# A leaky ramp on ScalarE in place of a byte comparison on VectorE, and a new order for the start of an attention and feed-forward kernel

## The chip, the cores and the metric

One core of one Trainium2 chip runs the whole program in one launch. The metric is the device time of that launch in microseconds (us). All matrix products are float32; a product with full precision is made of three products of 128x128 by up to 288 columns (high by high, low by high, high by low), since each operand is split into a part that TensorE keeps and a rest.

## What is computed

Memory attention (8 batches, 8 heads, 576 positions, 64 wide, 32 memory slots), then two feed-forward blocks:

```
a = softmax(phi, over 32 slots)          # [b, h, s, m]
k_m, v_m = a^T k, a^T v                  # [b, h, m, d]
x = softmax(q k_m^T / 8) v_m             # -> [b, s, 512]
xk = mu_k*x + (1-mu_k)*x_prev            # x_prev: x one position earlier
xr = mu_r*x + (1-mu_r)*x_prev
x2 = sigmoid(xr w_r) * (relu(xk w_k)^2 w_v)
u, v = relu(x2 w_in) halves;  v = layer_norm(v)
out = (u * (w_spatial v + b_spatial)) w_out
```

The weights arrive as 64-bit floats, bit for bit, and the kernel turns them into float32 itself.

## The kernel before

**Units.** The work goes through 16 half blocks `i` (batch `b`, half `hf` of 288 positions). In each, TensorE makes 8 key products (`w_k`, tiles W1h and W1l), 4 gate products (`w_r`, W2h and W2l) and 4 value products (`w_v`, W3h and W3l), L616 to L690; then the second feed-forward block follows (L699 on). Attention runs in 16 groups `i` of 4 heads (`att_step`, L212): a reduction and an exponential of phi, the memory's keys and values (L235, 20 rows of small products), their transposition (L273), the scores (L285), a second softmax on VectorE and ScalarE (L291 to L317), and the products that write x (L337 to L342, tile xT).

**Weights.** `load_f64` (L109) takes one unit of 128x512 64-bit numbers: a DMA into one of four staging buffers (st0, st1 and two halves of xT1, in turn), a scaling on ScalarE of the upper words (L123), the lowest bits of the lower words by ScalarE (L127, first 6 units) or VectorE (L129), a comparison on VectorE of the sign's byte, which writes 128 or 0 into the byte that holds the sign (L131), a shift and OR on VectorE (L135), a rounded copy on ScalarE (L141) and the rest on VectorE (L142). w_k has 8 units, w_r 4, w_v 8; 12 more (w_in, w_out) come in the middle of the run.

**Order.** Up to the first half block the text is written out by the string `ORDER` (L34): capitals and small letters of A, C, K, Q (group 0) and B, D, L, R (group 1) are input loads, `w` is one unit of w_k, `a` and `b` take the two first attention groups one stage on. `FIRST_BLOCK` (L37) does the same inside half block 0. From then on `pump` (L357) is called 20 times per half block, and takes the following attention groups on by 0, 2 or 1 steps. A scheduler then moves instructions within each engine's queue, and each queue runs strictly in its order. DMAs of this kernel all go through SyncE's queue, in its order too.

Of the kernel before, what the change touches and what calls it, by code (L numbers as in the profile page):

```python
# [8 lines left out]
F32 = mybir.dt.float32  # L9
F32R = mybir.dt.float32r  # L10
U32 = mybir.dt.uint32
U8 = mybir.dt.uint8
ACTF = mybir.ActivationFunctionType
ALU = mybir.AluOpType
# [5 lines left out]
DM, DFF = 512, 1024  # L20
# [8 lines left out]
KC = DM // 128  # L29
# [1 line left out]

ORDER = "AICKMBDwLQRwwqwraaawaaabbbabaabbwbbwbw"  # L34


FIRST_BLOCK = ["arxxab", "b", "rxabr", "xab", "", "", "", "rv", "vvvv", "v", "", "vv"]  # L37
# [3 lines left out]
def kernel(  # L41
# [18 lines left out]
    nc = tc.nc  # L60
    scale = 1.0 / float(D) ** 0.5
# [44 lines left out]
    stages = []  # L106
    units = [0]

    def load_f64(src, wh=None, wl=None, raw=None):  # L109


        c, f = src.shape[1], src.shape[2] // 2
        buf = stages.pop(0)
        stages.append(buf)
        if isinstance(buf, str):
            buf = tile_of(buf, [128, 1024], U32)
        st = buf[:, 0:2 * c * f].rearrange("p (c f b) -> p c f b", c=c, b=2)
        nc.sync.dma_start(out=st.rearrange("p c f b -> p c (f b)"), in_=src)
        low, top = st[:, :, :, 0], st[:, :, :, 1]
        by = buf.bitcast(U8)[:, 0:8 * c * f].rearrange("p (c f b) -> p c f b", c=c, b=8)  # L120


        nc.scalar.activation(out=top.bitcast(F32), in_=top.bitcast(F32), func=ACTF.Copy, scale=2.0**-112)  # L123
        units[0] += 1
        if units[0] <= 6:

            nc.scalar.activation(out=low, in_=by[:, :, :, 3], func=ACTF.Copy, scale=2.0**-5, bias=-0.4999)  # L127
        else:
            nc.vector.tensor_scalar(out=low, in0=low, scalar1=29, scalar2=None, op0=ALU.logical_shift_right)  # L129

        nc.vector.tensor_scalar(  # L131
            out=by[:, :, :, 3], in0=by[:, :, :, 7], scalar1=128.0, scalar2=128.0, op0=ALU.is_ge, op1=ALU.mult
        )
        out = top if raw is None else raw.bitcast(U32)
        nc.vector.scalar_tensor_tensor(  # L135
            out=out, in0=top, scalar=3, in1=low, op0=ALU.logical_shift_left, op1=ALU.bitwise_or
        )
        v = out.bitcast(F32)
        if wh is None:
            return v  # L140
        nc.scalar.activation(out=wh, in_=v, func=ACTF.Copy)  # L141
        nc.vector.tensor_tensor(out=wl, in0=v, in1=wh.bitcast(F32), op=ALU.subtract)  # L142

    def weight(src, dst, n_c, width):

        chunks = src.bitcast(U32).rearrange("(c p) f -> p c f", p=128)
        for f0 in range(0, width, 128):
            for c in range(0, n_c, 4):
                load_f64(
                    chunks[:, c:c + 4, 2 * f0:2 * f0 + 256],  # L150
                    dst[0][:, c:c + 4, f0:f0 + 128], dst[1][:, c:c + 4, f0:f0 + 128],
                )
                yield
# [58 lines left out]
    def att_step(i):  # L212
        b, g = divmod(i, G)
        sp = space(i)
        pT, ph, kv, q, st, mx, rs, sm = sp.pT, sp.ph, sp.kv, sp.q, sp.st, sp.mx, sp.rs, sp.sm
# [10 lines left out]
            out=ph, in0=ph, in1=bc[:, None, :].to_broadcast([128, NT, 128]), op=ALU.subtract  # L226
# [6 lines left out]
        for t in range(NT):  # L233
            for j in range(HG):
                nc.tensor.matmul(  # L235
                    out=kvp[32 * j:32 * j + 32, :], lhsT=ph[:, t, 32 * j:32 * j + 32],
                    rhs=kv[:, t, j, :], start=(t == 0), stop=(t == NT - 1),
                )
            if t == 1:
                yield True  # L240
        nc.vector.tensor_scalar(out=rs, in0=kvp[:, 128:129], scalar1=1e-9, scalar2=None, op0=ALU.add)
        nc.vector.reciprocal(out=rs, in_=rs)

# [1 line left out]
            out=km.rearrange("p (e d) -> p e d", e=2), in0=kvp[:, None, 0:64].to_broadcast([128, 2, 64]),  # L245
            scalar1=rs, scalar2=None, op0=ALU.mult,
        )
        if wide:
            nc.vector.scalar_tensor_tensor(
                out=vb, in0=kvp[:, None, 64:128].to_broadcast([128, HG, 64]), scalar=rs,  # L250
                in1=mask_sb[:, 2:, None].to_broadcast([128, HG, 64]), op0=ALU.mult, op1=ALU.mult,
            )
            x = vb.rearrange("p (a j) d -> p a (j d)", a=2)
            split(x, vbh, vbl)
        else:
            x = vb[:, 0:2, :]
            nc.vector.scalar_tensor_tensor(
                out=x, in0=kvp[:, None, 64:128].to_broadcast([128, 2, 64]), scalar=rs,
                in1=mask_sb[:, 0:2, None].to_broadcast([128, 2, 64]), op0=ALU.mult, op1=ALU.mult,
            )  # L260
            x = x.rearrange("p a d -> p (a d)")
# [16 lines left out]
        for halves in ((0,), (1,)) if i < 2 else ((0, 1),):  # L278
# [4 lines left out]
            for j in range(HG):  # L283
                for hf in halves:
                    nc.tensor.matmul(  # L285
                        out=scs[hf][32 * j:32 * j + 32, :],
# [3 lines left out]
            for hf in halves:  # L290
                nc.vector.transpose(  # L291
                    out=st[:, hf * NBLK // 2:(hf + 1) * NBLK // 2, :].rearrange("p a m -> p (a m)"),
                    in_=scs[hf],
# [3 lines left out]
            if i > 0 and halves[-1] == 1:  # L297
# [4 lines left out]
                out=st[:, bl], in0=st[:, bl], in1=mx2[:, bl].to_broadcast([128, n_b, 32]), op=ALU.subtract  # L302
# [10 lines left out]
                out=st[:, bl], in0=st[:, bl], in1=sm[:, bl].to_broadcast([128, n_b, 32]), op=ALU.mult  # L313
# [6 lines left out]
            else:  # L320
                for pr in range(2):
# [4 lines left out]
                        out=ats[there, pr, :], in0=at[here], in1=h.bitcast(F32), op=ALU.subtract  # L326
# [5 lines left out]
            for pr in range(2):  # L332
                for hf in halves:
# [4 lines left out]
                    else:  # L338
                        gemm(xo, [(vbh[:, pr, :], ats[:, pr, s1]), (vbl[:, pr, :], ats[:, pr, s1])])
                    nc.scalar.activation(  # L340
                        out=xT[b][:, 2 * g + pr, 1 + hf * HB:1 + (hf + 1) * HB], in_=xo, func=ACTF.Copy
# [15 lines left out]
    def pump():  # L357
        n = slot[0]
        slot[0] += 1
        for _ in range(0 if n < 7 else 2 if n < 32 else 1):  # L360
            next(att, None)
        next(more[0], None)

# [5 lines left out]
    def prep_x(i, which, c):  # L369
        b, hf = divmod(i, 2)  # L370
        x32 = tile_of(next(x32_tags), [128, HB])
        n = which * KC + c

        nc.scalar.activation(
            out=x32, in_=xT[b][:, c, hf * HB:(hf + 1) * HB], func=ACTF.Copy,
            scale=mu_sb[:, 2 * KC + n:2 * KC + n + 1],
        )
        nc.vector.scalar_tensor_tensor(  # L378
            out=x32, in0=xT[b][:, c, 1 + hf * HB:1 + (hf + 1) * HB], scalar=mu_sb[:, n:n + 1], in1=x32,
            op0=ALU.mult, op1=ALU.add,  # L380
        )
        both = operand(n)[:, 0:2 * HB]
        h, lo = both[:, 0:HB], both[:, HB:]
        split(x32, h, lo)
        xs[i, which, c] = (h, lo)
# [17 lines left out]
    stages += ["st0", "st1"] + [spare[:, n, :] for n in range(2)]  # L403
    wk = pair("W1", [128, KC, DFF])
    wr = pair("W2", [128, KC, DM])
    w_k_steps = weight(w_k, wk, KC, DFF)
    w_r_steps = weight(w_r, wr, KC, DM)

    def load(n, i, late):
# [8 lines left out]
            pass  # L418

    for c in ORDER:  # L420
        if c == "w":
            next(w_k_steps)
        elif c in "ab":
            stage(first[c == "b"])
        elif c == "I":
            nc.sync.dma_start(out=ident_sb, in_=ident)
        elif c == "M":
            nc.sync.dma_start(out=mask_sb, in_=blockmask)
            nc.sync.dma_start(out=mu_sb[:, 0:2 * KC], in_=mu)
            nc.vector.tensor_scalar(  # L430
                out=mu_sb[:, 2 * KC:], in0=mu_sb[:, 0:2 * KC], scalar1=-1.0, scalar2=1.0,
                op0=ALU.mult, op1=ALU.add,
            )
        else:
            n, late = "ACKQBDLR".index(c.upper()), c.islower()
            load(n % 4, n // 4, late)
    for c in range(KC):
        prep_x(0, 0, c)

    wv = []  # L440

# [554 lines left out]
```

## Time and profile before

| | before |
|---|---|
| median of 3 runs | 1040.32 us (1038.41 to 1043.42) |
| the profiled execution | 1039.12 us, of which 1037.3 us span from its first to its last instruction |
| TensorE busy | 989.4 us, 95% of the span |
| VectorE busy | 693.3 us, 67% |
| ScalarE busy | 605.5 us, 58% |
| GpSimd busy | 117.3 us, 11% |
| DMA | 88.94 MB |
| mean granted TensorE clock | 0.997 |

The shares are means over stretches of different kinds: in the first twentieths of the span TensorE is partly idle and VectorE is full; from then on TensorE is nearly always busy. The rows further down go by stretch. A time is read as "start of the row, us, duration, us"; where an engine is full, the distance from one row's start to the next one's is what an instruction costs, since neighbours overlap by a little.

### The profile page before, as it was taken

To read this page: it belongs to the slowest core of one execution; us is meant where nothing else is said; L and a number is where in the kernel's file an instruction comes from. 1 tells how busy PE (TensorE), PEld (TensorE's weight loads), DVE (VectorE), ACT (ScalarE), POOL (GpSimd) and SP (SyncE) were. 2 spreads that over 40 slices of the span, in tenths; PEclk is the share of its full clock that TensorE was granted. 3 is DMA by queue.
4 is the path that set the end of the run, shared out by engine and by line. 5 is a ranking of instruction groups with operands and counts; after the bars stand their busy time and mean duration, and the time that the engine had idled before them with its cause. 6 is when DMAs were issued, how large, how long until landed. Compare 5 with 4: busy or idle time off the path is not lost.

```text
span 1037.3 us, 20311 instructions
## 1 busy us (share of the span) xinstructions
PE 989.4 (95%) x8080; PEld 957.8 (92%) x8080; DVE 693.3 (67%) x1558; ACT 605.5 (58%) x1287; POOL 117.3 (11%) x128
## 2 busy tenths in 40 slices
PE   3698999999999999999999999899999999999998
PEld 1387899999999999999999999899999999999998
DVE  3999956755674566567588557885665757575653
ACT  2797875675676568566766574655353534445342
POOL 0000000000000000000013022232232313132220
PEclk9999999999999999999999999899999999999999
DMA  9856622321332233223042212112110111111101
GB/s 258 260 155 205 203 80 64 113 88 55 108 111 88 58 110 105 75 66 105 7 145 64 74 44 84 39 55 65 36 61 30 59 35 53 40 59 46 54 24 46
DMA packets 67454, 88.94 MB, mean 86 GB/s; under 512 B 9504, under 2 KB 61088, under 8 KB 65312
## 3 DMA queue, kind: packets, MB, share of 16 engines
q1 hardware_dynamic: 67360, 87.65, 27.2%
q8 instruction: 63, 1.03, 0.4%
q14 instruction: 31, 0.25, 0.1%
HBM read 68.75 MB, written 18.87 MB: 84 GB/s over the span
## 4 chain that ended last, share of the span: by engine, by line
PE 81%; DVE 9%; DMA 4%; ACT 4%; issue 1%; SPq 1%; POOL 0%; ACTq 0%; POOLq 0%; DVEq 0%
PE bank L96 78%; PE bank L235 2%; DMA ATl<-in_qT 1%; DMA st<-in_w_in 1%; PE bank L285 1%; DVE xs L104 1%; DVE kl L104 1%; DMA ATh<-in_kv 1%; DVE st L131 1%; DVE xT L135 1%; DMA st<-in_w_v 0%; DVE xT L131 0%; ACT st L750 0%; ACT xs L103 0%; POOL st L558 0%
## 5 line engine op out<-in xcount | busy, mean ns | idle before, releaser
L96 PE MATMUL bank<-xs,W1h 128*128 128x288 f32 (+1 forms) x1496 | 251.9, 295 | 9.8 <-ACT xs L103 8.6
L96 PEld LDWEIGHTS bank<-xs,W1h 128*128 128x128 f32 x1496 | 214.4, 190 | 15.1 <-ACT xs L103 10.4
L96 PE MATMUL bank<-xs,W1l 128*128 128x288 f32 (+1 forms) x748 | 136.9, 292 | 0.0
L104 DVE TENSOR_TENSOR kl<-t,kh 128x576 fp32r<-128x576 f32 x64 | 49.1, 767 | 110.4 <-ACT kh L103 109.7
L96 PEld LDWEIGHTS bank<-xs,W1l 128*128 128x128 f32 x748 | 112.3, 190 | 0.0
L630 ACT ACTIVATE t<-bank 128x288 f32<-128x288 f32 x128 | 51.6, 403 | 78.3 <-PE bank L96 77.4
L767 DVE TENSOR_TENSOR st<-bank,st 128x256 f32<-128x256 f32 x90 | 37.5, 424 | 73.5 <-PE bank L96 64.9
L96 PE MATMUL bank<-kh,W3h 128*128 128x288 f32 x512 | 78.9, 295 | 6.2 <-ACT W3h L141 5.0
L96 PE MATMUL bank<-xs,W2h 128*128 128x288 f32 x512 | 84.2, 300 | 0.0
L96 PE MATMUL bank<-kh,W3l 128*128 128x288 f32 x512 | 81.3, 297 | 0.0
L96 PE MATMUL bank<-ATh,xs 128*128 128x256 f32 x472 | 75.1, 281 | 3.2 <-ACT st L770 3.1
L96 PEld LDWEIGHTS bank<-kh,W3h 128*128 128x128 f32 x512 | 71.1, 188 | 7.4 <-ACT W3h L141 5.9
L96 PE MATMUL bank<-kl,W3h 128*128 128x288 f32 x512 | 77.7, 294 | 0.0
L96 PEld LDWEIGHTS bank<-kh,W3l 128*128 128x128 f32 x512 | 71.3, 188 | 6.2 <-issue 6.0
L96 PEld LDWEIGHTS bank<-xs,W2h 128*128 128x128 f32 x512 | 72.6, 188 | 2.4 <-ACT t L630 2.2
L96 PEld LDWEIGHTS bank<-kl,W3h 128*128 128x128 f32 x512 | 71.0, 188 | 0.0
L96 PEld LDWEIGHTS bank<-ATh,xs 128*128 128x128 f32 x472 | 64.6, 191 | 3.7 <-ACT st L770 3.3
L104 DVE TENSOR_TENSOR xs<-st,xs 128x512 fp32r<-128x512 f32 x56 | 52.3, 935 | 16.1 <-ACT xs L103 16.1
L103 ACT ACTIVATE xs<-st 128x512 fp32r<-128x512 f32 x56 | 34.2, 630 | 46.0 <-POOL st L558 35.5
L103 ACT ACTIVATE kh<-bank 128x288 fp32r<-128x288 f32 x64 | 25.9, 406 | 50.9 <-DVE bank L887 50.9
L908 ACT ACTIVATE o<-bank 128x288 f32<-128x288 f32 x64 | 25.8, 404 | 45.2 <-PE bank L96 38.2
L331 POOL MEMSET xT<- 128x4 f32 x8 | 0.8, 105 | 445.0 <-DVE x32b L378 353.8
(242 smaller groups left out, 2217.4 us busy)
## 6 DMA issues: line engine op xcount, KB each, us to landing
ATh<-in_kv SPq DMA_DIRECT2D x15, 1300.0 KB, 6.1
out_T<-o SPq DMA_DIRECT2D x64, 144.0 KB, 1.7
ATl<-in_qT SPq DMA_DIRECT2D x30, 288.0 KB, 4.3
st<-x2d SPq DMA_DIRECT2D x32, 256.0 KB, 3.4
ATh<-in_phin SPq DMA_DIRECT2D x15, 320.0 KB, 3.0
x2d<-o SPq DMA_DIRECT2D x32, 144.0 KB, 2.0
ATh<-in_phiT SPq DMA_DIRECT2D x15, 288.0 KB, 2.8
st<-in_w_in SPq DMA_DIRECT2D x8, 512.0 KB, 4.0
```

What stands on the lines that cost most here:

```text
L96: nc.tensor.matmul(out=out, lhsT=pairs[i][0], rhs=pairs[i][1], start=i == 0, stop=i == n - 1)
L103: nc.scalar.activation(out=h, in_=x, func=ACTF.Copy)
L104: nc.vector.tensor_tensor(out=lo, in0=x, in1=h.bitcast(F32), op=ALU.subtract)
L131: nc.vector.tensor_scalar(out=by[:, :, :, 3], in0=by[:, :, :, 7], scalar1=128.0, scalar2=128.0, op0=ALU.is_ge, op1=ALU.mult)
L135: nc.vector.scalar_tensor_tensor(out=out, in0=top, scalar=3, in1=low, op0=ALU.logical_shift_left, op1=ALU.bitwise_or)
L235: nc.tensor.matmul(out=kvp[32 * j:32 * j + 32, :], lhsT=ph[:, t, 32 * j:32 * j + 32], rhs=kv[:, t, j, :], start=(t == 0), stop=(t == NT - 1),)
L285: nc.tensor.matmul(out=scs[hf][32 * j:32 * j + 32, :], lhsT=kmT[64 * hf:64 * hf + 64, 32 * j:32 * j + 32], rhs=q[64 * hf:64 * hf + 64, j, ...
L331: nc.gpsimd.memset(xT[b][:, :, 0:1], 0.0)
L630: nc.scalar.activation(out=ks[:, m % 2 * HB:(m % 2 + 1) * HB], in_=acc, func=ACTF.Relu)
L767: engine.tensor_tensor(out=dst, in0=x, in1=y, op=ALU.add)
L908: nc.scalar.activation(out=o, in_=acc, func=ACTF.Copy)
```

## The change

- The byte comparison (L131) is gone from all 32 units. ScalarE's scaling, which was a plain copy with a scale of 2^-112, becomes a leaky ramp with the same scale and a slope of -2^32 for negative numbers, so that the sign arrives in a bit that the following shift and OR puts in its place.
- The DMA of a unit (`fetch`) is separated from its conversion. `ORDER` names the DMAs of w_k (`W`) and the conversions (`w`) apart, and the four chunks of the first operand (`x`) as well. All conversions of w_k stand behind the two attention groups, and four loads of group 0 and 1 that came between or behind w_k's first units now come ahead of them.
- The stage border inside the 20 small key and value products (after `t == 1`) is taken out, so an attention group has one step less.
- `pump` takes 0 steps up to its 14th call (7th before), then 3 up to the 28th (2 up to the 32nd before), then 1.

```diff
-ORDER = "AICKMBDwLQRwwqwraaawaaabbbabaabbwbbwbw"
+ORDER = "AICKMQBDLRWWWWqraabbaaaabababxxbbbxxwwwwwwww"
...
-        nc.scalar.activation(out=top.bitcast(F32), in_=top.bitcast(F32), func=ACTF.Copy, scale=2.0**-112)
+        nc.scalar.activation(
+            out=top.bitcast(F32), in_=top.bitcast(F32), func=ACTF.Prelu, scale=2.0**-112, alpha=-(2.0**32)
+        )
...
-        nc.vector.tensor_scalar(
-            out=by[:, :, :, 3], in0=by[:, :, :, 7], scalar1=128.0, scalar2=128.0, op0=ALU.is_ge, op1=ALU.mult
-        )
...
-            if t == 1:
-                yield True
...
-        for _ in range(0 if n < 7 else 2 if n < 32 else 1):
+        for _ in range(0 if n < 14 else 3 if n < 28 else 1):
...
+        if c == "W":
+            fetch_w_k()
+        elif c == "w":
+            f0 = next(w_k_parts)
+            load_f64(fetched[f0 // 128], *(t[:, :, f0:f0 + 128] for t in wk))
+            fetch_w_k()
+        elif c == "x":
+            prep_x(0, 0, next(xk_chunks))
```

What this does to the queues is shown at three places. Lines of the changed kernel are 3 to 16 higher: its L118 is still the weights' DMA, L423 is L411 (loads of the first two groups), L138, L140 and L147 are L129, L135 and L142, L381 is L378, L695 is L679.

The first place is SyncE's queue at the start, before the change (ATh, ATl are group 0's tiles, W3h and kh group 1's; st0, st1, xT1 the staging buffers):

```order
L411 DMA ATh_78<-in_kv1 128x2600
L428 DMA mask_64<-in_blockmask 128x6
L429 DMA mu_65<-in_mu 128x8
L411 DMA W3h_80<-in_phiT 128x576
L411 DMA W3h_80<-in_phin 128x640
L118 DMA st0_100<-in_w_k 128x4x256
L411 DMA W3h_80<-in_kv1 128x2600
L411 DMA ATl_76<-in_qT 64x4x288
L411 DMA kh_77<-in_qT 64x4x288
L118 DMA st1_111<-in_w_k 128x4x256
```

And after it:

```order
L423 DMA ATh_78<-in_kv1 128x2600
L446 DMA mask_64<-in_blockmask 128x6
L447 DMA mu_65<-in_mu 128x8
L423 DMA ATl_76<-in_qT 64x4x288
L423 DMA W3h_80<-in_phiT 128x576
L423 DMA W3h_80<-in_phin 128x640
L423 DMA W3h_80<-in_kv1 128x2600
L423 DMA kh_77<-in_qT 64x4x288
L118 DMA st0_103<-in_w_k 128x4x256
L118 DMA st1_105<-in_w_k 128x4x256
```

The first unit of w_k went from ahead of group 1's keys and values, and of both queries, to behind them.

The second place is VectorE's queue where w_v's last two units are converted, before the change (xs0 to xs3 are operand chunks of the next half block, asp and ATl belong to attention group 2, o0 is the first product to be stored):

```order
L267 TENSOR_TENSOR asp_79<-ATl_76,asp_79 64x128
L268 TENSOR_TENSOR asp_79<-ATl_76,asp_79 64x128
L378 SCALAR_TENSOR_TENSOR x32b_715<-xT0_226,mu_65,x32b_715 128x288
L129 TENSOR_SCALAR xT1_85<-xT1_85 128x512 x2
L104 TENSOR_TENSOR xs3_718<-x32b_715,xs3_718 128x288
L131 TENSOR_SCALAR xT1_85<-xT1_85 128x512 x2
L135 SCALAR_TENSOR_TENSOR xT1_85<-xT1_85 128x512 x2
L291 STREAM_TRANSPOSE ATl_76<-bank4_751 128x288
L142 TENSOR_TENSOR W3l_555<-xT1_85,W3h_554 128x4x128 x2
L291 STREAM_TRANSPOSE ATl_76<-bank5_752 128x288
L677 TENSOR_TENSOR o0_783<-bank0_738,r_569 128x288
```

And after it:

```order
L138 TENSOR_SCALAR xT1_85<-xT1_85 128x512
L147 TENSOR_TENSOR W3l_543<-st1_618,W3h_542 128x4x128
L105 TENSOR_TENSOR xs3_662<-x32b_659,xs3_662 128x288
L140 SCALAR_TENSOR_TENSOR xT1_85<-xT1_85 128x512
L138 TENSOR_SCALAR xT1_85<-xT1_85 128x512
L381 SCALAR_TENSOR_TENSOR x32a_705<-xT0_197,mu_65,x32a_705 128x288
L140 SCALAR_TENSOR_TENSOR xT1_85<-xT1_85 128x512
L147 TENSOR_TENSOR W3l_543<-xT1_85,W3h_542 128x4x128
L105 TENSOR_TENSOR xs4_708<-x32a_705,xs4_708 128x288
L147 TENSOR_TENSOR W3l_543<-xT1_85,W3h_542 128x4x128
L693 TENSOR_TENSOR o1_741<-bank1_711,r_551 128x288
L381 SCALAR_TENSOR_TENSOR x32b_744<-xT0_197,mu_65,x32b_744 128x288
```

The comparisons are gone; group 2's values (the rows on asp) and its scores (the STREAM_TRANSPOSE) now stand behind w_v's last unit, and one more operand chunk (xs4) and the first stored product stand ahead of it.

The third place is SyncE's queue at w_v's last loads, before the change:

```order
L118 DMA xT1_85<-in_w_v 128x4x256
L118 DMA st0_612<-in_w_v 128x4x256
L210 DMA ATh_78<-in_phin 128x640
L118 DMA st1_640<-in_w_v 128x4x256
L118 DMA xT1_85<-in_w_v 128x4x256 x2
L210 DMA ATh_78<-in_kv1 128x2600
```

And after it (x2d is the buffer in device memory for x2):

```order
L118 DMA st0_591<-in_w_v 128x4x256
L118 DMA st1_618<-in_w_v 128x4x256
L695 DMA x2d0_68<-o0_702 128x288
L215 DMA ATh_78<-in_phiT 128x576
L118 DMA xT1_85<-in_w_v 128x4x256 x2
L215 DMA ATh_78<-in_phin 128x640
L215 DMA ATh_78<-in_kv1 128x2600
```

The last two loads of w_v now stand behind the store of the first value product, and so behind that product's multiplication on VectorE.

## Rows read from the trace of the kernel before

**Rows 1.** Stretches: busy us (instructions) of each engine, granted clock, DMA share, GB/s.
```profile
0.00:26.37 26.37, 8.21 (x92) 4.92 (x92) 9.89 (x25) 6.81 (x13) 0.31 (x5) 1.00 0.95 259
26.37:47.42 21.05, 11.18 (x45) 5.69 (x45) 20.37 (x45) 16.43 (x35) 0.00 (x0) 1.00 0.85 254
47.42:71.00 23.58, 23.27 (x153) 22.23 (x153) 23.54 (x54) 22.81 (x50) 0.00 (x0) 1.00 0.56 161
71.00:93.65 22.65, 15.62 (x149) 13.84 (x150) 22.11 (x52) 16.40 (x30) 0.10 (x1) 1.00 0.84 265
93.65:134.94 41.29, 40.32 (x375) 37.14 (x374) 39.50 (x92) 33.59 (x71) 0.10 (x1) 1.00 0.49 154
134.94:1037.30 902.36, 890.77 (x7272) 873.99 (x7270) 577.92 (x1296) 509.48 (x1093) 116.82 (x121) 1.00 0.21 67
```

**Rows 2.** What TensorE waited for from 28 to 94 us: total, times, longest.
```profile
PE bank L96 <- ACT xs L103: 8.6, 2, 5.6
PE bank L96 <- ACT W3h L141: 5.0, 3, 2.6
PE bank L235 <- ACT ATh L228: 2.1, 1, 2.1
```

**Rows 3.** Timeline of TensorE: start us, duration us, form, idle before.
```profile
47.42 1.04 PE L96 MATMUL bank<-xs,W1h 128*128 128x288 f32 x2 [5.61 <-ACT xs L103]
...
93.65 0.70 PE L96 MATMUL bank<-xs,W1h 128*128 128x288 f32 x4
...
134.94 0.30 PE L96 MATMUL bank<-xs,W1h 128*128 128x288 f32 x1
```

**Rows 4.** Timeline of VectorE while it is full.
```profile
38.32 0.75 DVE L131 TENSOR_SCALAR st<-st 128x512 uint8<-128x512 uint8 x1
38.85 0.51 DVE L317 STREAM_TRANSPOSE r<-r 128x288 f32<-128x288 f32 x1
39.27 0.66 DVE L142 TENSOR_TENSOR W1l<-st,W1h 128x512 fp32r<-128x512 f32 x1
39.84 0.69 DVE L135 SCALAR_TENSOR_TENSOR st<-st 128x512 uint32<-128x512 uint32 x1
```

**Rows 5.** Groups by form, 26 to 130 us: busy us, mean ns, idle before.
```profile
L131 DVE TENSOR_SCALAR st<-st 128x512 uint8<-128x512 uint8 x11 | 8.4, 760 | 0.0
L131 DVE TENSOR_SCALAR xT<-xT 128x512 uint8<-128x512 uint8 x10 | 7.2, 762 | 0.0
```

**Rows 6.** Line 131 in the stretch behind 130 us: ns, first and last start.
```profile
L131 DVE TENSOR_SCALAR st<-st x10: 739/752/1679, 523.2 to 594.0; 128x512 uint8<-128x512 uint8 x10
```

**Rows 7.** Timeline of VectorE at the end of w_v's conversion.
```profile
84.61 0.22 DVE L266 CAST asp<-asp 64x128 fp32r<-64x128 f32 x1
...
86.28 0.52 DVE L378 SCALAR_TENSOR_TENSOR x32b<-xT,mu,x32b 128x288 f32<-128x288 f32 x1
...
90.07 0.48 DVE L291 STREAM_TRANSPOSE ATl<-bank 128x288 f32<-128x288 f32 x1
90.47 1.25 DVE L142 TENSOR_TENSOR W3l<-xT,W3h 128x512 fp32r<-128x512 f32 x2
91.64 0.48 DVE L291 STREAM_TRANSPOSE ATl<-bank 128x288 f32<-128x288 f32 x1
```

**Rows 8.** ScalarE's groups by form, 26 to 130 us.
```profile
L123 ACT ACTIVATE xT<-xT 128x512 f32<-128x512 f32 x10 | 6.8, 681 | 1.4 <-DMA xT<-in_w_k 1.1 <-DMA xT<-in_w_v 0.4
L632 ACT ACTIVATE t<-t 128x576 f32<-128x576 f32 x8 | 5.4, 680 | 0.1
L651 ACT ACT_TABLE_LOAD x3 | 3.8, 1283 | 0.1
L651 ACT ACTIVATE r<-bank 128x288 f32<-128x288 f32 x8 | 3.1, 402 | 0.1
```

**Rows 9.** Timeline of SyncE's queue: start, us until the next could issue.
```profile
5.85 0.67 SPq L118 DMA_DIRECT2D st<-in_w_k  x1
...
75.97 4.02 SPq L118 DMA_DIRECT2D xT<-in_w_v  x2
```

More of the change, by code (lines that the diff above doesn't have):

```diff
@@ L107, with fetch @@
     units = [0]
-    def load_f64(src, wh=None, wl=None, raw=None):
+    def fetch(src):
         c, f = src.shape[1], src.shape[2] // 2
@@ L118, in load_f64 @@
         nc.sync.dma_start(out=st.rearrange("p c f b -> p c (f b)"), in_=src)
+        return buf, st, c, f
+    def load_f64(src, wh=None, wl=None, raw=None):
+        buf, st, c, f = src if isinstance(src, tuple) else fetch(src)
         low, top = st[:, :, :, 0], st[:, :, :, 1]
         by = buf.bitcast(U8)[:, 0:8 * c * f].rearrange("p (c f b) -> p c f b", c=c, b=8)
-        nc.scalar.activation(out=top.bitcast(F32), in_=top.bitcast(F32), func=ACTF.Copy, scale=2.0**-112)
+        nc.scalar.activation(
+            out=top.bitcast(F32), in_=top.bitcast(F32), func=ACTF.Prelu, scale=2.0**-112, alpha=-(2.0**32)
+        )
         units[0] += 1
@@ L405, with fetch_w_k @@
     wr = pair("W2", [128, KC, DM])
-    w_k_steps = weight(w_k, wk, KC, DFF)
+    w_k_src = w_k.bitcast(U32).rearrange("(c p) f -> p c f", p=128)
+    fetched = []
+    def fetch_w_k():
+        f0 = 256 * len(fetched)
+        if f0 < 2 * DFF:
+            fetched.append(fetch(w_k_src[:, :, f0:f0 + 256]))
+    w_k_parts = iter(range(0, DFF, 128))
+    xk_chunks = iter(range(KC))
     w_r_steps = weight(w_r, wr, KC, DM)
@@ L420 @@
     for c in ORDER:
-        if c == "w":
-            next(w_k_steps)
+        if c == "W":
[6 more added lines that the diff above has]
+            prep_x(0, 0, next(xk_chunks))
         elif c in "ab":
@@ L436 @@
             load(n % 4, n // 4, late)
-    for c in range(KC):
-        prep_x(0, 0, c)
     wv = []
```

## Prediction

> **What bounds the kernel now.** I read the table of stretches first [rows 1], since the shares of the whole span mix two regimes. Behind 134.94 us TensorE is busy 890.8 of 902.4 us: 11.6 us idle in seven eighths of the run. In front of 93.65 us it is busy 58.3 us (8.2 + 11.2 + 23.3 + 15.6) and idle 35.4. So this change can win time only in the first tenth, and what it wins there reaches the end of the run, because everything behind is a queue of products that TensorE works off without a pause.
>
> Inside that tenth the same rows show who is full. From 26.37 to 93.65 us VectorE is busy 20.37 + 23.54 + 22.11 = 66.0 of 67.3 us. The list of TensorE's waits says what it lacked there: operand chunks (8.6 us, up to 47.42), units of w_v (5.0 us) and attention group 2's exponential, which stands in TensorE's queue ahead of value products (2.1 us) [rows 2, 3]. The engines named are ScalarE's, but what ScalarE had to work on came late from VectorE. So the stretch from 26 to 94 us is VectorE's queue, and it ends with the remainder of w_v's last units, 90.47 to 91.64 [rows 7]; the value products of half block 0 end 2.0 us later, at 93.65, where half block 1 begins [rows 3].
>
> ScalarE is close behind: 22.81 of 23.58 us between 47.42 and 71.00, 55.6 of 67.3 over the whole [rows 1]. DMA was busy 0.95 and 0.85 of the first two stretches.
>
> **The change part by part.**
>
> *The comparison.* Where VectorE is full, it costs the distance to the next start: 38.32 to 38.85, 0.53 us [rows 4], not the 0.76 of its duration [rows 5]. Of the 20 units of the three weights that this stretch serves, one comparison runs before 26.37, while VectorE is mostly idle, and gains nothing; 19 lie in the full stretch: 19 x 0.535 = **-10.2 us**. Two more start behind 94 us and ten between 523 and 594 [rows 5, 6], where TensorE is full: 0, for TensorE's products cover them. The bounds are 19 x 0.50 and 19 x 0.59, which I judge from neighbours in the same timeline: 9.5 to 11.2.
>
> *The leaky ramp.* No row shows one. The scaling takes 0.68 us for 512 numbers, a square 0.68 us for 576 [rows 8]: two functions at about the same rate. By the square's rate 512 numbers would take 0.60 us; I bound the ramp there and as far above the copy's row, at 0.76: from 20 x -0.08 to 20 x +0.08, or 1.6 us of ScalarE's time either way. I take 0, as it is the same instruction with another function. The changed program has no load of a function table at any of these scalings; in the start it has two such loads up to w_v's end where it had three, -1.28 us for ScalarE [rows 8], and two more in all (33 for 31) later, under a full TensorE. The Trainium skill ("ScalarE: Activation LUTs", "Step-by-step: what each stage is for") says that one number per cycle passes whatever the function is; no run here shows it for this ramp. The same page ("What ACT_TABLE_LOAD costs") counts 1283 ns for a load and some 1380 ns for draining with it, 2.66 us. The trace agrees with the first figure and shows no second one: eight gate results, three of them right behind a load, waited 0.1 us together [rows 8]. By the page the saved load would be 2.7 us instead of 1.3.
>
> *Attention pushed back.* Up to the end of w_v VectorE no longer does group 2's values (the six rows from 84.61 to 86.28, 1.7 us, and four short ones ahead of them, about 0.6) nor its first transposition (90.07 to 90.47, 0.4) [rows 7]: -2.7 us. In their place it now does group 3's reduction, the first stored product and one more operand chunk, estimated at 0.45 each for four instructions of the size of those in [rows 4], 1.8 us. Net **-0.9**, bounds -2.7 and 0.
>
> *Attention first, weights later.* The first unit of w_k was asked for at 5.85 us [rows 9]. Now two queries and group 1's keys and values (288 + 1300 + 288 KB, 1.92 MB by the shapes) go ahead of it: at 259 GB/s [rows 1] it lands 7.4 us later, an estimate. VectorE had 16.5 idle us before 26.37 [rows 1] and fills them with both groups' first softmax; counting down its queue, the conversions start near 29 us, with some 3 us more attention done than before. Net **+0.3**; bounds -2 (group 1's half no longer waits behind conversions) and +4.
>
> *Hand-over.* Each unit passes ScalarE, VectorE, ScalarE, VectorE. With VectorE's part shortened, ScalarE's 55.6 us of the stretch, less 1.3 for the table and some 1 for group 2, stand against VectorE's 66.0 - 10.2 - 0.9 = 54.9. Two engines equally full that feed each other lose time; before, ScalarE lost 11.7 us beside a full VectorE. I take **+3**, bounds 0 and +7. The third place of the queues adds to it: w_v's last two loads now wait for the first value product to be stored. Before, the second of them went out near 80.0 (75.97 + 4.02) and w_v was done 11.7 us later [rows 7, 9]; I expect them near 73 now, which gives 84.7 by the same distance.
>
> Sum up to w_v's last remainder: -10.2 - 0.9 + 0.3 + 3 = -7.8, so 91.64 becomes 83.8, in line with 84.7.
>
> *Behind it.* The products take the same 2.0 us to follow. By then TensorE has also made the first key group of half block 1 (12 products of 0.122 us, 890.77 / 7272 [rows 1], 1.5) but not group 2's scores (about 0.7): **-0.8**. From there to 134.94 VectorE was busy 39.5 of 41.3 us: it has the postponed 2.7 us to do there as well, and 1.07 less for two comparisons. Attention runs 3 steps per call, so its small products meet results that are not ready: the products of group 2 stand in the middle of a key group, behind a chain of about 11 us on VectorE. TensorE has about 10 us of key products to cover it: **+1**, bounds 0 and +5. One step less per attention group only moves later groups earlier under a full TensorE. The cluster of 20 key products itself costs nothing: the same products, without a border.
>
> Total: -7.8 - 0.8 + 1 = -7.6 us. Against the profiled execution, 1039.12 us (span 1037.3, so 1.8 around it, which stays), this gives 1031.5; the median of the runs, 1.2 higher, would give 1032.7. I say **1032**.
>
> **Rivals.**
>
> *A. No hand-over loss.* VectorE stays as full as it was and the dense attention costs nothing: -10.2 - 0.9 - 0.8 = -11.9, with the front's -2 at most -14: 1025 to 1028. For it: VectorE lost only 1.3 us in 67 before. Against: ScalarE had slack then.
>
> *B. ScalarE becomes the bound.* It keeps the same waits as before, 11.7 us beside about 53 us of work: w_v ends near 29 + 60 = 89, and 4 us or less remain: 1035 to 1039. For it: 22.81 of 23.58 us already. Against: most of its waits were for VectorE and go with it.
>
> *C. The gain is given back in half block 1.* Dense attention and a VectorE that is already 96% busy there make the first chunk of half block 2 late. It decides when TensorE waits more than 7 us between the end of w_v's products and half block 2: 1037 to 1041. Against: before, TensorE idled only 1.0 us in that stretch.
>
> *D. Slower: the weights' arrival is the bound.* DMA was busy 0.95 and 0.85 in front, and the first weights land 7.4 us later. If conversions were fed by arrivals and not by VectorE, all would shift by that, and the removed comparisons would shorten nothing: 1039.1 + 7.4 = 1046.5. It decides when ScalarE's waits for weights' DMAs, now 1.4 us for the ten units through xT's buffers [rows 8], exceed about 10. Against: they are small, and from 47 to 71 us the DMA share is 0.56.
>
> **How the numbers follow.** A difference under 0.5% (5.2 us) is about what a measurement of this kernel can't tell from none. My forecast, 4 to 11 us won, has 0.62; A 0.10, B 0.12, C 0.09, D 0.07. Faster by over 0.5%: A, nearly all of the forecast (0.60) and a third of B, together 0.74. Slower by over 0.5%: D and a little of C, 0.08. The rest, 0.18, is the same. The range runs from A's middle, 1026, to the middle of B and C, 1038; it leaves out a part of A, half of C and D.
>
> **What would show it.** VectorE's comparison gone, and its other rows at the same distances. ScalarE's scaling at 0.68 us; at 0.75 or more the ramp has a price. The conversions' first VectorE row near 29 us, TensorE's main products from about 40 instead of 47.4, w_v's last remainder near 84, half block 1 at 86 (a first key group earlier), half block 2 near 127 instead of 134.9. From there equal distances to the end. I am wrong if w_v ends before 81 or behind 88, if TensorE waits for DMAs of weights, or if the stretch up to half block 2 grows by over 5 us of waits for attention.

## The result, and the profile after

The changed kernel took 1031.75 us (median of 6 runs, 1030.23 to 1035.93) beside 1040.61 us of the kernel before on the same chip (1038.41 to 1043.42). The ratio is 0.9912, with a 95% interval of 0.9893 to 0.9930: faster by 0.9%, 8.9 us. The forecast was 1032. Its sum, though, was made of terms that the runs do not bear out one by one. The profiled execution took 1030.61 us, span 1028.8.

The changed kernel's stretches from 39.44 us on, columns as in [rows 1]:

```profile
39.44:54.00 14.56, 13.13 (x88) 12.65 (x87) 13.37 (x33) 13.81 (x31) 0.00 (x0) 1.00 1.02 298
54.00:67.44 13.44, 11.65 (x58) 10.43 (x59) 12.76 (x26) 12.84 (x26) 0.00 (x0) 0.75 0.59 191
67.44:87.37 19.93, 16.84 (x145) 14.97 (x144) 17.69 (x39) 15.47 (x30) 0.10 (x1) 1.00 0.81 271
87.37:129.44 42.07, 41.51 (x384) 36.74 (x383) 37.89 (x92) 35.42 (x72) 0.11 (x1) 1.00 0.55 167
129.44:1028.80 899.36, 888.25 (x7272) 874.87 (x7270) 574.75 (x1289) 515.23 (x1096) 115.80 (x121) 1.00 0.21 67
```

The last three rows answer to the last three of [rows 1]: value products of half block 0, half block 1, and the rest. The value products of half block 0 end at 87.37 instead of 93.65 (-6.3), half block 2 begins at 129.44 instead of 134.94 (-5.5), and from there to the end it is 899.36 instead of 902.36 us (-3.0), with the same 7272 products. So 5.5 of the 8.5 us come from the front, where all 7.6 were expected, and 3.0 from a stretch that was to stay as it was. VectorE is no longer the only full engine in front: from 39.44 to 67.44 ScalarE is as full (26.65 of 28.00 us, VectorE 26.13).

What TensorE waited for from 28 to 90 us; this answers to [rows 2]:

```profile
PE bank L97 <- ACT W1h L146: 4.0, 2, 3.6
PE bank L97 <- ACT W2h L146: 2.2, 2, 1.4
```

It now waits first for weights of w_k and w_r rather than for operand chunks: the weights come behind attention. VectorE's timeline at the first conversion and around w_v's last units, which answers to [rows 7]:

```profile
29.57 1.29 DVE L140 SCALAR_TENSOR_TENSOR st<-st 128x512 uint32<-128x512 uint32 x2
...
73.94 1.28 DVE L147 TENSOR_TENSOR W3l<-xT,W3h 128x512 fp32r<-128x512 f32 x2
...
80.49 0.43 DVE L138 TENSOR_SCALAR xT<-xT 128x512 uint32<-128x512 uint32 x1 [1.96 <-DMA xT<-in_w_v]
...
84.74 0.69 DVE L147 TENSOR_TENSOR W3l<-xT,W3h 128x512 fp32r<-128x512 f32 x1
85.35 0.45 DVE L693 TENSOR_TENSOR o<-bank,r 128x288 f32<-128x288 f32 x1
```

The row behind the last remainder, which started at 91.64 before, starts at 85.35 here. The ramp on ScalarE, in groups by form as in [rows 8], from 26 to 130 us:

```profile
L130 ACT ACTIVATE st<-st 128x512 f32<-128x512 f32 x12 | 8.2, 681 | 0.3 <-DMA st<-in_w_r 0.3
L130 ACT ACTIVATE xT<-xT 128x512 f32<-128x512 f32 x10 | 6.9, 687 | 1.8 <-DMA xT<-in_w_v 1.3 <-DMA xT<-in_w_k 0.4
```

681 and 687 ns, where the plain scaling had 681: the ramp costs ScalarE nothing that shows. SyncE's queue at w_v's last two loads:

```profile
73.39 0.34 SPq L695 DMA_DIRECT2D x2d<-o  x1
...
74.65 0.98 SPq L118 DMA_DIRECT2D xT<-in_w_v  x2
```

They follow the store, as the order had shown, near the 73 us that were expected; but they went out 1.3 us behind it, when the two remainders at 73.94 on the same tile xT were being made.

In half block 1, TensorE's timeline where attention groups 2 and 3 meet:

```profile
100.66 0.67 PE L288 MATMUL bank<-ATl,ATh 64*32 64x288 f32 x2
101.26 0.79 PE L97 MATMUL bank<-asp 128*128 128x288 f32 x4
101.99 0.67 PE L288 MATMUL bank<-ATl,ATh 64*32 64x288 f32 x2
102.58 0.80 PE L97 MATMUL bank<-asp 128*128 128x288 f32 x4
103.32 0.70 PE L288 MATMUL bank<-ATl,ATh 64*32 64x288 f32 x12
103.95 0.80 PE L97 MATMUL bank<-xs,W1h 128*128 128x288 f32 x4
```

Sixteen scores and eight full products take 3.29 us here (100.66 to 103.95), since they alternate: two scores alone take the 0.67 us that twelve take in 0.70. No list of waits shows this. In the kernel before the sixteen stand together:

```profile
106.94 0.72 PE L285 MATMUL bank<-ATl,ATh 64*32 64x288 f32 x16 [0.15 <-ACT ATh L274]
```

### The profile page after: what moved, and what is told of

The parts are those of the page before. It is cut to its first block, busy times and chain, and to the rows that moved or that the text cites. A ratio compares the mean times of both kernels' runs of the same rounds, so it can differ in the third digit from the quotient of the medians.

```text
span 1028.8 us, 20280 instructions
## 1 busy us (share of the span) xinstructions
PE 990.6 (96%) x8080; PEld 961.1 (93%) x8080; DVE 678.1 (66%) x1526; ACT 610.8 (59%) x1289; POOL 116.3 (11%) x128
## 4 chain that ended last, share of the span: by engine, by line
PE 82%; DVE 6%; DMA 5%; ACT 4%; issue 1%; POOL 0%; SPq 0%; ACTq 0%; DVEq 0%; POOLq 0%
PE bank L97 79%; PE bank L240 2%; DMA st<-in_w_in 2%; PE bank L288 1%; DMA ATh<-in_kv 1%; DMA st<-in_w_r 1%; DVE xs L105 1%; DMA xT<-in_w_v 1%; DMA xT<-in_w_k 1%; DMA st<-in_w_v 0%; DVE kl L105 0%; DVE xT L140 0%; ACT xs L104 0%; POOL st L574 0%; ACT t L648 0%
## 5 line engine op out<-in xcount | busy, mean ns | idle before, releaser
L97 PE MATMUL bank<-xs,W1h 128*128 128x288 f32 (+1 forms) x1496 | 248.3, 295 | 5.8 <-ACT W1h L146 4.0
```

The source lines that it names most:

```text
L97: nc.tensor.matmul(out=out, lhsT=pairs[i][0], rhs=pairs[i][1], start=i == 0, stop=i == n - 1)
```

## Experiments

Two marks are read in each trace: the end of VectorE's last w_v row, and the first product of half block 2. "Behind" is the span less that product's start. Each kernel also ran 6 or 12 times. The marks come from one execution each, and executions of one kernel lie 1.6 to 7 us apart, so medians carry the verdicts. (The kernel of experiment 10 was profiled in an execution of 1034.81 us, 4.4 over its median; its marks may be late by that.)

| kernel | order | sign | border | pump | w_v ends | half block 2 | behind | median us |
|---|---|---|---|---|---|---|---|---|
| before | old | comparison | middle | early | 91.72 | 134.94 | 902.4 | 1040.6 |
| after | new | ramp | none | late | 85.43 | 129.44 | 899.4 | 1031.75 |
| 1 ramp only | old | ramp | middle | early | 87.60 | 130.78 | 900.8 | 1033.43 |
| 2 comparison back | new | comparison | none | late | 92.67 | 140.59 | 905.9 | 1048.38 |
| 3 border moved | old | comparison | behind | early | 94.08 | 137.32 | 899.2 | 1038.11 |
| 4 border back | new | ramp | middle | late | 84.69 | 128.89 | 902.9 | 1033.59 |
| 5 pump back | new | ramp | none | early | 90.50 | 135.23 | 898.2 | 1034.58 |
| 6 fifth buffer | new | ramp | none | late | 84.88 | 131.51 | 900.8 | 1032.34 |
| 7 compared twice | old | two comparisons | middle | early | 103.91 | 149.06 | 903.9 | 1052.89 |
| 8 order alone | new | comparison | middle | early | 97.33 | 142.57 | 902.8 | 1047.27 |
| 9 border behind | new | ramp | behind | late | 84.81 | 128.84 | 898.9 | 1029.64 |
| 10 ramp and cluster | old | ramp | behind | early | 90.59 | 133.73 | 899.3 | 1030.40 |
| 11 the same, late pump | old | ramp | behind | late | 85.31 | 130.45 | 898.1 | 1029.94 |
| 12 late comparisons | new | both | none | late | 86.18 | 130.40 | 905.8 | 1037.82 |

**1. The ramp alone, in the kernel before.**

```diff
-        nc.scalar.activation(out=top.bitcast(F32), in_=top.bitcast(F32), func=ACTF.Copy, scale=2.0**-112)
+        nc.scalar.activation(
+            out=top.bitcast(F32), in_=top.bitcast(F32), func=ACTF.Prelu, scale=2.0**-112, alpha=-(2.0**32)
+        )
...
-        nc.vector.tensor_scalar(
-            out=by[:, :, :, 3], in0=by[:, :, :, 7], scalar1=128.0, scalar2=128.0, op0=ALU.is_ge, op1=ALU.mult
-        )
```

> The kernel before with the leaky ramp in place of scaling plus comparison, order, border and pump as before. Theory (VectorE's queue bounds the front, so that the comparison's time there comes back less a loss at the hand-over): w_v's last remainder 6 to 8 us earlier than 91.64, half block 2 at 128 to 130, equal distances behind it, 1033 to 1036 us in all. Rival (the order of the loads makes the difference, and the comparison hid beside ScalarE and the DMAs): less than 2.5 us won, 1038 us or more.

Measured: 1033.43 us, ratio 0.9933 (0.9918 to 0.9948): the theory holds for the total. At the marks it is less than expected: w_v ends 4.1 us earlier (6 to 8 were expected), half block 2 starts 4.2 earlier, 1.5 more come behind. What VectorE waited for from 26 to 92 us in this kernel:

```profile
DVE ATl L290 <- PE bank L284: 3.3, 1, 3.3
DVE x32a L377 <- ACT x32a L373: 1.4, 1, 1.4
DVE xs L104 <- ACT xs L103: 0.9, 1, 0.9
```

With two shorter waits these are 6.3 us, against 1.3 that it stood idle between 26.37 and 93.65 before [rows 1]. In the old order the removed work, 10.2 us by the prediction's distances, brings 4.1: 5.0 us more than before go into waits for group 0's scores (L284) and for ScalarE.

**2. The comparison put back into the kernel after** (the same diff, reversed).

> The kernel after with plain scaling and the byte comparison on VectorE put back, new order, pump and no border. Theory: the front is 5 to 8 us longer, the rest is as in the kernel after, 1037 to 1040 us. Rival (order): 1033 us or less. If the order itself was worth nothing and the cluster 3 us, this kernel stands some 3 us under the kernel before.

Measured: 1048.38 us, ratio 1.0073 (1.0056 to 1.0089) to the kernel before. Both theories fail on the high side: without the ramp the rest of the change is not a gain but a loss of 7.5 us, and within this order the ramp is worth 16.6 us, not 7.4.

**3. The border moved, in the kernel before, to behind the key and value products.**

```diff
-            if t == 1:
-                yield True
+        yield True
```

> The kernel before, with the stage border moved from the middle of the key and value products to behind them: the same number of steps in each attention group, the same pump, but one cluster of 40 small products per group instead of 16 and 24. Theory (each cluster costs TensorE a fixed time at its border): 0.24 us less in each of some 13 groups under a full TensorE, -2.5 to -3.5 us, 1037 to 1038 us. Rival, the prediction's own term (a border costs nothing, and the 3 us behind half block 2 come from the faster pace of 19 steps): 1040 to 1041 us.

Measured: 1038.11 us, ratio 0.9982 (0.9967 to 0.9996); 899.2 us behind half block 2 instead of 902.4. The theory holds for that stretch, and the prediction's "costs nothing" does not. The total is at the edge of the expected range: by its interval 0.4 to 3.4 us are won, and in the profiled execution half block 2 starts 2.4 us later than before; whether by the edit or by the execution is not shown.

**4. The border in the middle put back into the kernel after** (with it go one `a` and one `b` more in `ORDER`).

```diff
-ORDER = "AICKMQBDLRWWWWqraabbaaaabababxxbbbxxwwwwwwww"
+ORDER = "AICKMQBDLRWWWWqraabbaaaaabbababxxbbbxxwwwwwwww"
...
+            if t == 1:
+                yield True
```

> The kernel after with the border in the middle of the key and value products put back, and one more a and b in the order so that the start is recorded as it was: 20 steps a group again, two clusters. Theory (cluster): 2.5 to 3.5 us slower than the kernel after, 1034 to 1035.5 us, all of it behind half block 2. Rival (a border costs nothing): 1031 to 1032.5 us. Together with the border moved in the kernel before: if only this one moves, it was the number of steps and not the cluster.

Measured: 1033.59 us, +1.8 over the kernel after, less than the theory's 2.5 to 3.5, and the intervals of the two ratios overlap (0.9926 to 0.9959 here). Behind half block 2 it is 902.9 instead of 899.4 us, as the theory said, but the front is 0.6 us shorter. Group of the small products from 170 to 480 us in this kernel:

```profile
L240 PE MATMUL bank<-ATh 128*32 128x130 f32 x360 | 13.7, 279 | 0.0
```

and in the kernel of experiment 9, where they are one cluster:

```profile
L240 PE MATMUL bank<-ATh 128*32 128x130 f32 x360 | 11.8, 276 | 0.0
```

The same 360 products of nine groups, 1.9 us less: 0.21 us a group. TensorE's timeline of one group, in the kernel with the border in the middle:

```profile
183.54 0.65 PE L240 MATMUL bank<-ATh 128*32 128x130 f32 x16
184.12 0.80 PE L97 MATMUL bank<-xs,W2h 128*128 128x288 f32 x4
...
185.29 0.69 PE L97 MATMUL bank<-xs,W2h 128*128 128x288 f32 x4
185.91 0.87 PE L240 MATMUL bank<-ATh 128*32 128x130 f32 x24
186.72 1.32 PE L97 MATMUL bank<-kh,W3h 128*128 128x288 f32 x8
```

and with one cluster:

```profile
183.10 1.32 PE L240 MATMUL bank<-ATh 128*32 128x130 f32 x40
184.35 0.80 PE L97 MATMUL bank<-xs,W2h 128*128 128x288 f32 x4
```

16 and 24 products cost 0.58 and 0.81 us up to the next row, 40 cost 1.25; and the full products behind a border start with a slower first four (0.80 for 0.69). The Trainium skill ("TensorEngine Tiling (Array Packing)", "Key Properties") says that a change of tiling mode drains TensorE. The trace is in line with it: two changes of mode less save 0.14 us of small products and 0.11 us of full ones, some 0.25 us a group.

**5. Before's pump in the kernel after.**

```diff
-        for _ in range(0 if n < 14 else 3 if n < 28 else 1):
+        for _ in range(0 if n < 7 else 2 if n < 32 else 1):
```

> The kernel after with the pump schedule of before (0 steps up to the 7th call, 2 up to the 32nd). First results of half blocks 1 and 2 in the kernel after: 89.1 and 131.8 us, 42.7 apart, before 40.0. Theory (the attention that is postponed out of half block 0 is given back in half block 1): half block 1 lasts 40 to 40.7 us and starts 1 to 2.7 us later, so the total stays between 1031 and 1033 us. Rival (the new order of the start lengthens half block 1): it still lasts 42 us or more and starts later too, 1033 to 1035 us.

Measured: 1034.58 us, +2.8 over the kernel after, though the intervals of the two ratios overlap (0.9918 to 0.9958 here). Half block 1 lasted 42.4 us from first result to first result (94.67 to 137.03): the rival holds. In these two executions postponing takes 5.1 us off w_v's end (90.50 to 85.43); the prediction had 0.9 for it.

**6. A fifth staging buffer for w_v.**

```diff
         wv.extend(pair("W3", [128, FC, DM]))
+        stages.insert(0, tile_of("asp", [128, 1024], U32))
...
```

The rest of the edit makes attention's tile `asp` anew for the groups from 2 on.

> The kernel after with a fifth staging buffer for w_v, in the place of group 0's attention tile, which is free then. Theory (the last two loads of w_v wait for a buffer, not for the store ahead of them, and that costs VectorE its 2.0 us wait at 80.5): they go out 2 to 3 us earlier, the wait goes, w_v's last remainder starts at 82.5 to 83.2 instead of 84.74, 1029.5 to 1030.7 us. Rival (VectorE and ScalarE are the bound, the wait comes back elsewhere): 1031.3 us or more.

Measured: 1032.34 us, no gain. The last two loads went out 3.3 us earlier, and ahead of the store:

```profile
71.37 1.57 SPq L118 DMA_DIRECT2D st<-in_w_v  x2
```

VectorE's wait for them is gone, but w_v ends only 0.55 us earlier:

```profile
79.02 0.69 DVE L147 TENSOR_TENSOR W3l<-asp,W3h 128x512 fp32r<-128x512 f32 x1 [0.63 <-ACT W3h L146]
...
83.45 0.82 DVE L230 TENSOR_TENSOR ATh<-ATh,bank 128x640 f32<-128x640 f32 x1
84.19 0.69 DVE L147 TENSOR_TENSOR W3l<-st,W3h 128x512 fp32r<-128x512 f32 x1
```

The rival holds: VectorE now waits for ScalarE's rounded copy instead, and takes a row of attention (L230) ahead of w_v's last one. Half block 2 starts 2.1 us later than in the kernel after; whether the moved attention tile has a part in that was not separated.

**7. The comparison twice in the first twenty units, in the kernel before.**

```diff
+        if units[0] <= 20:
+            nc.vector.tensor_scalar(
+                out=by[:, :, :, 3], in0=by[:, :, :, 7], scalar1=128.0, scalar2=128.0, op0=ALU.is_ge, op1=ALU.mult
+            )
```

> The kernel before with the comparison done twice in each of the first 20 units (same operands, same result). Taking it away in the old order brought w_v's last remainder only 4.1 us forward. Theory (with the comparisons VectorE is the only bound, without them its neighbours bind as well): the second comparison costs its full distance, 19 x 0.53 = 10 us, w_v's last remainder at 100 to 102 us, 1049 to 1052 us in all. Rival (a comparison is half hidden whichever way): 4 to 5 us, 1044 to 1046 us.

Measured: 1052.89 us, ratio 1.0113 (1.0091 to 1.0136), +12.2, and w_v's end 12.2 later. In VectorE's timeline the last remainder stands at

```profile
102.66 1.25 DVE L146 TENSOR_TENSOR W3l<-xT,W3h 128x512 fp32r<-128x512 f32 x2
```

The theory holds, a little beyond its range: adding costs the whole distance and more (12.2 / 19 = 0.64 us each), taking away in the same order returned 4.1 at w_v's end. VectorE is the bound, with little room behind it.

**8. The new order alone.** Scaling, comparison, border and pump as before; `ORDER` (as in experiment 4), `fetch` and the four `x` are new.

> The kernel before with the new order of the start alone: scaling and comparison, border and pump as before. The kernel after with the comparison put back took 1048.4 us: half block 1's first result came 0.6 us later than before, half block 2's 6.0 us later. Theory (the order costs little by itself, and with a full VectorE the postponed attention costs 5 us): half block 1's first result at 96 to 98, half block 2's at 136 to 138, 1039.5 to 1042 us. Rival (the order is what costs, as long as VectorE has the comparisons to do): half block 2's at 141 or later, 1044 us or more.

Measured: 1047.27 us, ratio 1.0063 (1.0046 to 1.0079). The rival holds: by itself the new order costs 6.0 us. VectorE's timeline, first comparison and last remainder of w_v:

```profile
30.52 0.73 DVE L137 TENSOR_SCALAR st<-st 128x512 uint8<-128x512 uint8 x1
...
96.08 1.25 DVE L148 TENSOR_TENSOR W3l<-xT,W3h 128x512 fp32r<-128x512 f32 x2
```

Before, VectorE was full with conversions from 26.37 on [rows 1], one unit of w_k had been finished ahead of that (its last row started at 18.25), and the last remainder started at 90.47 [rows 7]. The new order starts 4.2 us later with one unit more to do, and ends 5.6 later. VectorE's busy time in the windows 0 to 30 and 30 to 90 us shows what is missing. Before:

```profile
0.00:30.00 30.00, 11.18 (x105) 5.97 (x106) 13.52 (x33) 9.19 (x17) 0.31 (x5) 1.00 0.97 252
30.00:90.00 60.00, 43.79 (x311) 37.40 (x310) 58.73 (x132) 51.75 (x104) 0.00 (x0) 1.00 0.72 228
```

and with the new order alone:

```profile
0.00:30.00 30.00, 11.64 (x106) 6.67 (x106) 11.98 (x31) 8.56 (x18) 0.31 (x5) 1.00 0.91 242
30.00:90.00 60.00, 45.33 (x273) 38.78 (x273) 56.75 (x121) 48.36 (x97) 0.00 (x0) 0.89 0.65 210
```

1.5 us less work in the first window (13.52 to 11.98), and 2.0 less in the second, where ScalarE does 3.4 less as well.

**9. The border behind the products in the kernel after** (one cluster, 20 steps).

> The kernel after with a stage border behind the key and value products (one cluster of 40, but 20 steps a group). Beside the kernel with the border in the middle (1033.6 us) it differs by the cluster alone. Theory (the cluster is worth 3 us): 1030 to 1031 us. Rival (it is the faster pace of 19 steps): 1033 to 1034 us.

Measured: 1029.64 us, ratio 0.9895 (0.9879 to 0.9911), 4.0 us under experiment 4, and the two intervals lie apart. The theory holds. It is also 2.1 us under the kernel after, with the same 899 us behind half block 2; the intervals of the two ratios overlap.

**10. Old order and old pump, with ramp and cluster.**

> The kernel before with the ramp and with the border behind the key and value products; order and pump as before. Theory (the ramp's gain and the cluster's are in different stretches and add up): 1033.4 less 3 = 1030 to 1031 us. Rival (the cluster only pays where the attention is early enough): 1032.5 us or more.

Measured: 1030.40 us, ratio 0.9901 (0.9878 to 0.9924). The theory holds for the total: -7.4 (experiment 1) and -2.7 (experiment 3) make -10.1, measured -10.3. Behind half block 2 they do not add up: 1.5 and 3.2 us were won there one by one, 3.1 together.

**11. The same with the late pump.**

> The same with the pump of the kernel after: ramp, cluster and postponed attention, without the new order. Theory (postponing takes 4 to 5 us of VectorE's work out of the way of w_v's conversion in either order, and the order itself costs 3 us): w_v's last remainder at 82 to 83, half block 2's first result at 127 to 129, 1025 to 1027.5 us, less than the 1029.6 of the same kernel with the new order. Rival (the order is what makes room for postponing): 1029 us or more.

Measured: 1029.94 us, ratio 0.9893 (0.9870 to 0.9916). The theory fails: the median gains 0.5 us. In the traces w_v ends 5.3 us earlier than in experiment 10, but that one's execution was 4.4 us over its median and this one's 0.4, so how much of the 5.3 is the pump's is not shown. Beside ramp, cluster and late pump the new order is worth nothing that can be told from zero: experiment 9, which differs from this one by the order alone, took 1029.64.

**12. Comparisons for the late twelve units alone, in the kernel after.**

```diff
+        units[0] += 1
+        late = units[0] > 20
+        if late:
+            nc.scalar.activation(out=top.bitcast(F32), in_=top.bitcast(F32), func=ACTF.Copy, scale=2.0**-112)
+        else:
...
+        if late:
+            nc.vector.tensor_scalar(
+                out=by[:, :, :, 3], in0=by[:, :, :, 7], scalar1=128.0, scalar2=128.0, op0=ALU.is_ge, op1=ALU.mult
+            )
```

> The kernel after with scaling and comparison put back for the twelve units that come late (w_in and w_out), the ramp kept for the first twenty. Theory (two comparisons beside GpSimd's work cost 1.7 us each and stand ahead of a value product's multiplication, for which TensorE then waits 3 us and falls to the lower clock): in the kernel with all comparisons put back this stretch, from the first result of half block 12 to that of 15, took 107.9 us instead of 101.5; here 104.5 to 108 us, and 1034.5 to 1038 us in all. Rival, the prediction's own term (comparisons under a full TensorE cost nothing): 101 to 102.5 us there, 1031 to 1032.5 in all.

Measured: 1037.82 us, +6.1. From the first key result of half block 12 (489.6) to that of 15 (597.6) it took 108.0 us, and 101.5 in the kernel after. VectorE's timeline there, with GpSimd's four subtractions running from 557.02 to 562.49:

```profile
558.69 2.69 DVE L142 TENSOR_SCALAR st<-st 128x512 uint32<-128x512 uint32 x2 [1.81 <-DMA st<-in_w_out]
561.29 2.37 DVE L144 TENSOR_SCALAR st<-st 128x512 uint8<-128x512 uint8 x2
563.45 0.84 DVE L701 TENSOR_TENSOR o<-bank,r 128x288 f32<-128x288 f32 x2
```

and TensorE's:

```profile
563.98 0.99 PE L97 MATMUL bank<-xs,W1h 128*128 128x288 f32 x4 [3.86 <-DVE o L701]
...
565.73 2.12 PE L97 MATMUL bank<-xs,W1h 128*128 128x288 f32 x8
...
568.26 1.23 PE L97 MATMUL bank<-xs,W1h 128*128 128x288 f32 x8
```

The theory holds. A pair of shifts and a pair of comparisons stand ahead of the multiplication that frees a PSUM bank; TensorE waits 3.86 us and then works at its lower level of 1.2 GHz (granted clock 0.60 from 563.98 to 568.26), eight products in 2.12 us instead of 1.23. In the kernel before and in experiment 8, with the same comparisons, it did not wait for such a multiplication; in experiment 2 it did, for 3.2 us. So it is the new pace of attention that brings the two together, and the ramp takes the comparisons away; whether the missing step or the later pump does it was not tried.

## Why the prediction was right, and where its steps were not

**What bounds the front.** Right: VectorE's queue does (experiment 7), with ScalarE and group 0's scores close behind it in the old order (experiment 1).

**The comparison, -10.2.** Right in the new order: the comparisons of the first twenty units cost 10.6 us by the medians (experiments 2 and 12), 6.5 at w_v's end and 10.2 at half block 2 (140.59 to 130.40). In the old order they cost 4.2 at half block 2 (experiment 1).

**The ramp, 0.** Right, 681 and 687 ns, with two table loads up to w_v's end instead of three, as forecast.

**Hand-over, +3.** About right at w_v's end, for which it was meant, in the new order: of 10.2 us 6.5 came back there, 3.7 less. The rest came back by half block 2, which the prediction did not expect. In the old order 6 us were lost (10.2 less 4.1) and stayed lost. The reason named at w_v's last loads was wrong: VectorE did wait 2.0 us for them, but they went out when their buffers came free, 1.3 us behind the store, and sending them 3.3 us earlier gained nothing (experiment 6).

**Attention first, +0.3, and the adding up.** The first step that failed. The prediction gave each part one price and added these. With the comparisons in place the order alone cost 6.0 us (experiment 8), outside its bounds of -2 and +4; beside ramp, cluster and late pump it cost nothing (experiments 9 and 11), inside them. Likewise the ramp is worth 7.4 us in the old order and 16.6 in the new one, 6.1 of these at the late units (experiment 12). Where conversions would start was right (29.57 for 29), but the prediction set some 3 us of attention done earlier against the late start, and left out the unit of w_k that VectorE had converted while it was idle.

**Attention pushed back, -0.9.** Too small at w_v's end in the traces (-5.1 in experiment 5, beyond the bound of -2.7), but -2.8 and -0.5 in the medians (experiments 5 and 11): part of it is given back.

**Sum up to w_v, and behind it.** -6.3 for -7.8 forecast; half block 2 -5.5 for -7.6, so +0.8 between them instead of +0.2. TensorE did not wait there. From the first key result of half block 1 to that of half block 2:

```profile
89.07:131.84 42.77, 42.21 (x390) 37.73 (x375) 38.46 (x90) 34.93 (x71) 0.11 (x1) 1.00 0.53 162
```

and before:

```profile
96.69:136.74 40.05, 39.08 (x364) 35.76 (x363) 37.48 (x88) 31.94 (x70) 0.10 (x1) 1.00 0.49 154
```

The stretch is longer because it holds more products, 390 for 364, with TensorE idle for 0.6 us (1.0 before), and because some of them alternate as shown above. Without new order and late pump it is 40.1 us with 370 products (experiments 1 and 10); with the early pump and no alternation it is still 42.4 us with 381 (experiment 5), with the old order and the late pump 43.9 us with 418 (experiment 11).

**The cluster, 0, and equal distances behind half block 2.** The second step that failed. "The same products, without a border" left out that TensorE pays at each change between small and full products, some 0.25 us a group for the two that a border adds: -2.7, -3.0 and -4.0 us in the medians (experiments 3, 10, and 9 against 4).

**Late comparisons, 0.** The cover of "a full TensorE" held in the old schedule but for 1.5 us (experiment 1, 902.4 to 900.8), and not in the new one: 6.1 us (experiment 12). The prediction priced an edit by a cover that another edit of the same change moves.

One way from the kernel before to the kernel after, by medians: ramp -7.4, cluster -3.0, late pump -0.5, new order -0.3 (1029.94 to 1029.64), one step less +2.1. These are steps of one chain, so they must come near the 8.9 measured (they make 9.1); the two of 0.5 us and less can't be told from nothing, and along another way, with the order first, the prices are others. The total of the forecast was right by luck: two errors had opposite signs, 2.1 us too much expected up to half block 2, and 3.0 too little behind it. None of the rivals A to D came about as described; C, the gain given back in half block 1, was named with TensorE waiting over 7 us there, and it was idle for 0.6.

Two things stay open: why the new order and the late pump each bring more products into half block 1's stretch (the time between its first key result and the next half block's), and whether 19 steps a group are really slower than 20 with one cluster.

## What to carry to other kernels

Work removed from a full engine can come back in part only, when the engine then waits for its neighbours (4.1 of 10.2 us in experiment 1); adding the same work and taking it away are two different experiments. A term of nothing "because it is covered" holds for one schedule: if the same change moves the cover, price it again. Small products of another tile shape cost less side by side on TensorE here, and a list of waits does not show what their borders cost.

## What the hardware showed that was not expected

**VectorE beside GpSimd.** While GpSimd subtracted, VectorE's rows took up to three times as long: a multiply-add of 0.51 us 1.54 (kernel after), a shift of 0.43 us 1.35 and a comparison of 0.76 us 1.19 (2.69 and 2.37 for two, experiment 12). GpSimd's own rows took 1.3 to 1.5 us each. In the kernel after:

```profile
553.74 1.47 POOL L491 TENSOR_TENSOR asp<-asp,xT 128x512 f32<-128x512 f32 x1
...
553.98 1.54 DVE L381 SCALAR_TENSOR_TENSOR x32a<-xT,mu,x32a 128x288 f32<-128x288 f32 x1
```

The Trainium skill ("SBUF — State Buffer", "SBUF: two separate sides") calls the ports that both use an exclusive lock, and names VectorE's instructions with two inputs in SBUF, or in a two-port mode. The trace agrees for the multiply-add; that the shift and the comparison, with one input, run in such a mode no run here shows.

**A granted clock of 1.00 with products at the lower pace.** TensorE's window from 40 to 50 us in experiment 1, and then in the kernel before:

```profile
40.00:50.00 10.00, 5.35 (x20) 4.91 (x21) 9.89 (x24) 8.43 (x20) 0.00 (x0) 0.50 0.92 265
```

```profile
40.00:50.00 10.00, 4.39 (x16) 3.82 (x17) 10.00 (x22) 7.10 (x15) 0.00 (x0) 1.00 0.92 278
```

0.50 is the level of 1.2 GHz, 1.00 that of 2.4 GHz. Yet a product took 0.27 us in both windows (5.35 / 20 and 4.39 / 16), while at 93.65 in the kernel before four took 0.70 together [rows 3]. So the column alone does not tell how fast TensorE worked in front, and experiment 1 was not slower there than the kernel before. In experiment 1 the column had begun to fall between 20 and 30 us, with TensorE busy for 6.3 of 10 us. It did not do so in every execution: two of the six had a mean granted clock of 0.98 and took 1032.44 and 1033.33 us, the other four had 0.997 or 0.998 and took 1033.25 to 1034.03. No cost shows in these times. In the kernel after the column reads 0.75 from 54.00 to 67.44, after a stretch with TensorE busy for 13.13 of 14.56 us.
